# Two staging slots of their own in the second gate/up pass of a linear-attention and SwiGLU kernel

## The chip, the cores and the metric

The kernel runs on one core of a Trainium2 chip. A core has a matrix engine (TensorE, PE in the profile; its weight loads are PEld), a vector engine (VectorE, DVE), a scalar engine (ScalarE, ACT), a general engine (GpSimd, POOL) and a queue engine that only starts transfers (SyncE, SP). Each runs its own instructions in order, and they wait for each other by semaphores. Sixteen DMA engines move data between the chip's memory (DRAM) and the core's on-chip memory (SBUF); PSUM holds the sums of matmuls. The metric is device microseconds (us) of one execution, and the median over several.

## The reference

The input x is 2048 tokens by 1024 features in bf16. With xn, its layer norm, the kernel computes a linear attention block s and a SwiGLU block, and joins them:

```
xn = layernorm(x)
q, k, v = split(xn @ wqkv)                 # 32 heads of 32
phi(t) = where(t > 0, t + 1, exp(t)) + 1e-6
s = ((phi(q) @ (phi(k)^T @ v)) / (phi(q) . sum phi(k) + 1e-6)) @ wo
b = (silu(xn @ w_gate) * (xn @ w_up)) @ w_down      # inner width 3584
out = x + s * silu(b)
```

The change touches only b: its products with w_gate and w_up for the second half of the tokens, and the preparation of w_down for the product behind it.

## The kernel before

The large products go through a seven-product scheme for 2 x 2 blocks (Strassen-Winograd): sums of operand blocks are formed beside the matmuls, and seven block products replace eight. The tokens are taken in two passes of 1024. Each pass has a gate/up part of 28 units and then a down part (the product with w_down).

**Gate/up.** A unit is one weight key: a gate (g) or an up (u) slice of 256 columns, alternating, so that keys 0 to 27 are g0, u0, g1, u1 and so on. `emit_a` starts a key with 16 matmuls (four of the products), `emit_b` ends it with 12. On PE the first part of key i+1 stands ahead of the second part of key i. `emit_evac` then brings the results through DVE and ACT into hT, four rows of which make a group j of seven groups (NQ).

**Weights.** A packed key (both halves and the sums of weight blocks) is 1024 KB; SP loads it (L263) into one of eight slots of the pool wgu (`w_slot`, L215 to L216). Slots are given out as they come free. `load_w_to(n)` starts all loads up to key n. In the second pass it runs ahead by five keys up to unit 16 and by six behind it (L1697).

**The down part of the second pass** (`emit_down_m`) applies the seven products once over, as products M1 to M7, and for M1, M2 and M4 the scheme once more inside (`l2_M`, `l2_p`). These inner products need sums of weight blocks and sums of hT blocks:

- For M1 and M4, the weight sums are made in the second gate/up pass. `l2_load` (L1102) takes a slot with `w_slot()` and starts four DMAs of 128 KB (L1111) that bring two groups of blocks (the last load of each M brings one). A unit later, `l2_sums` (L1134) does four subtractions on POOL (L1144) and starts, from POOL, the store of all seven blocks to DRAM (L1145; `l` in the profile is the tensor l2_drams). There are eight such turns, at the odd units 1 to 15 (L1737). M2's were made in the first pass (`l2_early`).
- The hT sums are made by `l2_lhs` (L1160) on POOL, four operations for each group j: for M1 into two slots of wgu kept in `r_spare` (taken at units 17 and 18, L1735 to L1736), for M2 into tiles that the first pass leaves over (`x_spare`, `kept` in the profile). Both run from unit 18 on, one group j of M1 and one of M2 per unit (L1739 to L1742). The last group of M1 is in `emit_evac` of the last key, that of M2 behind the loop.

**Input and output.** `io_load` (L1184) starts two loads (x and s of one tile, L1191 and L1192) into one of five io tiles; `fin` finishes a tile, starts its store (from POOL in the first pass, L1202) and calls `io_load` for a later one. Three `fin` of the first pass are left over and run at the ends of units 0, 1 and 2 of the second pass (`deferred`, L1743).

**Order.** PE, DVE, ACT and POOL issue in source order throughout (`manual_schedule`). SP is in source order in the attention phases; in the gate/up and down phases a planner orders its transfers by a model of when their buffers come free.

Of the kernel before, what the change touches and what calls it, by code (L numbers as in the profile page):

```python
# [21 lines left out]
def kernel(  # L22
# [11 lines left out]
    nc = tc.nc  # L34
# [155 lines left out]
    M_ORDER = (1, 2, 7, 6, 5, 4, 3)  # L190
    L2 = (1, 2, 4)
    L2_ORDER = (1, 2, 5, 6, 7, 4, 3)
    NQ = NFG // 2
    CH = CW // 2
    l2_drams = {}
# [19 lines left out]
    def w_slot():  # L215
        return wgu.tile([P, 2, DC, FW], BF16, name="w_sb", tag="pk")  # L216
# [52 lines left out]
    def load_w_to(n):  # L269
        while w_next[0] < min(n, len(w_seq)):  # L270
            load_w()
# [680 lines left out]
    with ExitStack() as p3:  # L952
# [145 lines left out]

        l2_q = deque((M, j) for M in L2 if M != 2 for j in range(0, NQ, 2))
        l2_live = deque()  # L1100

        def l2_load():  # L1102
            M, j0 = l2_q.popleft()
            kd, q = M_PACK[M]
            t = w_slot()
            v = t[:].rearrange("p h a b -> p (h a b)").rearrange("p (b j n) -> p b j n", b=8, n=CH)
            js = range(j0, min(j0 + 2, NQ))
            for j in js:
                for k, b0, b1 in ((0, 0, 7), (1, 1, 6)):
                    src = wd_drams[j][0 if kd == "a" else 1][:, k, q].rearrange("p (c n) -> p c n", n=CH)  # L1110
                    nc.sync.dma_start(out=v[:, b0:b1 + 1:b1 - b0, j - j0, :], in_=src)  # L1111
            l2_live.append((M, js, v))
# [31 lines left out]
                nc.gpsimd.tensor_tensor(out=b(o_), in0=b(a_), in1=b(b_), op=ALU.subtract)  # L1144
            nc.gpsimd.dma_start(out=l2_drams[M][:, :, js.start:js.stop, :], in_=v[:, 0:7, 0:n_, :])  # L1145

        x_spare, r_spare = [], []

        def l2_bufs(M):
            v = [x[:].rearrange("p a b -> p (a b)").bitcast(F16) for x in x_spare]  # L1150
            if M == 1:
# [23 lines left out]
        for p in passes:  # L1175
# [4 lines left out]
            for hf in (1, 0):  # L1180
                for t in (2 * hf, 2 * hf + 1):
                    fq += [(p, t + TPB, 0), (p, t, 1), (p, t, 0)]

        def io_load(after=None):  # L1184
            if not fq:
                return
            p, t, cc = key = fq.pop(0)
            r0 = p * TB2 + t * P
            pool, tg = (sp, "S%d" % len(fq)) if len(fq) < 3 else (iop, "io")
            io = pool.tile([P, 2, CW], BF16, name="io", tag=tg)  # L1190
            gate([nc.sync.dma_start(out=io[:, 0, :], in_=x2[r0:r0 + P, cc * CW:(cc + 1) * CW]),  # L1191
                  nc.sync.dma_start(out=io[:, 1, :], in_=s_dram[r0:r0 + P, cc * CW:(cc + 1) * CW])],  # L1192
                 after, sync=True)
            io_tiles[key] = io
# [418 lines left out]
        base = 0  # L1613
        for pi, p in enumerate(passes):
            h = hp.tile([P, FC, TB2], BF16, name="hT", tag="hT")
            keys = [(p, kd, fg) for fg in range(NFG) for kd in ("g", "u")]
            n = len(keys)
            first = pi == 0
            last_pass = pi == NPASS - 1

            if first:
                first_gate[0] = marks[("S", NB - 1, 0)]

            def raw(j):
                return 0 <= j < n and keys[j] in raw_keys

            def pipe(j):
                if raw(j):
                    emit_st0(keys[j], w_tiles[keys[j]])

            def pipe1(k, i):
                if raw(k):
                    emit_st1(keys[k], grp[keys[i + 1]][4][:, 0:1])

            def pipe2(j):
                if raw(j):
                    t = w_tiles[keys[j]]
                    emit_st2(keys[j], t, later=j == n - 1)
                    emit_lk(keys[j][2])
                    if j < n - 1:  # L1640
                        emit_T(keys[j], t)
                    raw_keys.discard(keys[j])

            wd_live = {}

            def wd_pipe(i):
                if (i - 3) % 3 == 0 and i // 3 - 1 in wd_live:
                    key, t = wd_live[i // 3 - 1]
                    w = raw_view(key, t)
                    nc.scalar.activation(out=w, in_=w, func=ACT.Copy, scale=cs_all[:, kcol(key):kcol(key) + 1])  # L1650
                if (i - 1) % 3 == 0 and (i - 1) // 3 in wd_live:
                    emit_st0(*wd_live[(i - 1) // 3])

            def wd_pipe1(i):
                if (i - 2) % 3 == 0 and (i - 2) // 3 in wd_live:
                    emit_st1(wd_live[(i - 2) // 3][0], grp[keys[i + 1]][4][:, 1:2])

            def wd_pipe2(i):
                m, r = divmod(i + 1, 3)
                if r == 1 and m - 1 in wd_live:  # L1660
                    emit_T(*wd_live[m - 1])
                elif r == 0:
                    if m - 1 in wd_live:
                        emit_st2(*wd_live[m - 1], later=True)
                    if NWE + m < NFG:
                        t = w_slot()
                        load_wd(t, NWE + m)
                        wd_live[m] = ((p, "w", NWE + m), t)

            def more_S(m):  # L1670
                if first:
                    scale_h(h, 2 * m, nc.scalar)
                    scale_h(h, 2 * m + 1, nc.vector)
                emit_hs(h, 0, m, nc.vector)

            def next_S(m):
                emit_hs(h, 1, m, nc.vector)

            def tail():
                emit_hs(h, 0, 2, nc.vector)  # L1680
                if first:
                    scale_h(h, 7, nc.scalar)
                emit_hs(h, 0, 3, nc.vector)

            na0 = 6 if first else 8
            l2_j = 0
            load_w_to(base + na0)
            if first:
                wd_pipe2(-1)
            emit_a(keys[0])  # L1690
            emit_c22(keys[0])
            first_gate[0] = None
            for i in range(n):
                if first:
                    load_w_to(base + i + (na0 if i < n - 7 else 8 if i > n - 6 else 7))
                else:
                    load_w_to(base + i + (5 if i < 17 else 6))  # L1697
                if i + 1 < n:
                    emit_a(keys[i + 1])
                    emit_c22(keys[i + 1])  # L1700
                for j in (range(5) if i == 0 else (i + 4,) if i != n - 6 else ()):
                    pipe(j)
                if first:
                    wd_pipe(i)
                    for k in {n - 4: (0,), n - 3: (2, 4), n - 2: (5, 6)}.get(i, ()):
                        scale_h(h, k, nc.scalar)
                mb = emit_b(keys[i])
                if first and i in range(n - 6, n - 1):
                    io_load(mb)
                pipe1(i + (4 if i == n - 5 else 3), i)  # L1710
                if first:
                    wd_pipe1(i)
                if not last_pass:
                    if i == n - 2:
                        emit_hs(h, 0, 0, nc.gpsimd)
                    if i == n - 1:
                        emit_hs(h, 0, 1, nc.vector)
                emit_evac(keys[i], h, tail if i == n - 1 and not last_pass else None)
                pipe2(i + (4 if i == n - 5 else 3))
                if first:  # L1720
                    wd_pipe2(i)
                    if i == 5:
                        emit_lk(0)
                    if i == n - 5:
                        emit_lam()
                    elif i == n - 4:
                        emit_sc(keys[-1], w_tiles[keys[-1]])
                        emit_T(keys[-1], w_tiles[keys[-1]])
                        scale_h(h, 1, nc.vector)
                    elif i == n - 3:  # L1730
                        scale_h(h, 3, nc.vector)
                if not first:
                    if l2_live:
                        l2_sums()
                    if i in (17, 18):  # L1735
                        r_spare.append(w_slot())  # L1736
                    if i % 2 == 1 and l2_q:  # L1737
                        l2_load()
                    if i >= 18 and 4 * l2_j + 4 <= i:  # L1739
                        l2_lhs(1, quads(h, 0, 0), l2_j, nc.gpsimd)  # L1740
                        l2_lhs(2, quads(h, 1, 0), l2_j, nc.gpsimd)
                        l2_j += 1  # L1742
                if deferred:  # L1743
                    deferred.pop(0)()
            base += n
            if last_pass:
                l2_lhs(2, quads(h, 1, 0), NQ - 1, nc.gpsimd)
                emit_down_m(p, h, base)
            else:
                emit_down(p, h, base, last_pass, more_S, next_S)  # L1750
            base += 2 * NWA
# [32 lines left out]
```

## Time and profile before

| | us |
|---|---|
| runs | 755.99, 756.44, 761.65 |
| median | 756.44 |
| profiled execution | 756.18 |
| its span | 754.4 |
| PE busy in it | 745.8 (99%) |
| DVE / POOL / ACT busy | 581.4 / 399.8 / 381.1 |
| second gate/up pass on PE | 498.5 to 668.7 |
| down part behind it | from 668.7 |
| granted TensorE clock (share of full speed) | 0.999 |

The span runs from the first to the last instruction of the profiled execution. A timeline row has start, duration, engine, line, operation and tiles; consecutive ones of a kind are merged, with their number behind the x. SPq and POOLq are the transfers that an engine starts; a transfer's own time is in the chain's rows that begin with DMA. A row of waits has the waiting engine and line, what it waited for, the total, the number of waits and the longest.

### The profile page before, as it was taken

To read this page: it belongs to the slowest core of one execution; us is meant where nothing else is said; L and a number is where in the kernel's file an instruction comes from. 1 tells how busy PE (TensorE), PEld (TensorE's weight loads), DVE (VectorE), ACT (ScalarE), POOL (GpSimd) and SP (SyncE) were. 2 spreads that over 40 slices of the span, in tenths; PEclk is the share of its full clock that TensorE was granted. 3 is DMA by queue.
4 is the path that set the end of the run, shared out by engine and by line. 5 is a ranking of instruction groups with operands and counts; after the bars stand their busy time and mean duration, and the time that the engine had idled before them with its cause. 6 is when DMAs were issued, how large, how long until landed. Compare 5 with 4: busy or idle time off the path is not lost.

```text
span 754.4 us, 11075 instructions
## 1 busy us (share of the span) xinstructions
PE 745.8 (99%) x3857; PEld 360.8 (48%) x3857; DVE 581.4 (77%) x1040; ACT 381.1 (51%) x545; POOL 399.8 (53%) x500
## 2 busy tenths in 40 slices
PE   8999999999999999999999999999999999999997
PEld 3544444454454444444444444444444444467464
DVE  6687787887697788888889785468776877687966
ACT  5677776889956575656658311132323222232023
POOL 2444799998540266868585021811542569434900
PEclk9999999999999999999999999999999999999999
DMA  9967799879779668878799228789786768479652
GB/s 318 304 146 139 228 332 298 303 158 271 206 190 296 231 214 301 295 279 316 273 323 409 111 65 306 222 295 339 258 306 222 281 206 344 147 258 318 209 161 77
DMA packets 129160, 187.77 MB, mean 249 GB/s; under 512 B 36208, under 2 KB 104176, under 8 KB 119376
## 3 DMA queue, kind: packets, MB, share of 16 engines
q1 hardware_dynamic: 121760, 156.00, 63.9%
q0 software_dynamic: 5904, 28.58, 9.9%
q10 hardware_dynamic: 1440, 2.49, 1.1%
q8 instruction: 30, 0.49, 0.3%
q14 instruction: 26, 0.21, 0.1%
HBM read 119.47 MB, written 60.23 MB: 238 GB/s over the span
## 4 chain that ended last, share of the span: by engine, by line
PE 84%; DMA 7%; POOL 3%; DVE 2%; issue 2%; ACT 1%; SPq 1%; POOLq 0%; DVEq 0%; ACTq 0%
PE zw L966 19%; PE kv_ps L554 15%; PE xb L966 10%; PE q_ps L183 6%; PE dzw L1228 6%; PE dm L1430 6%; PE yb L966 5%; PE dm L1466 4%; PE dx L1228 3%; DMA l<-w_sb 3%; PE fx L816 3%; DMA w_sb<-wd 3%; PE s_ps L774 3%; POOL w_sb L1144 2%; PE dy L1228 2%
## 5 line engine op out<-in xcount | busy, mean ns | idle before, releaser
L966 PEld LDWEIGHTS <-w_sb 128*128 128x128 f16 (+1 forms) x1568 | 152.1, 98 | 183.8 <-DMA w_sb<-pk_u 1.3
L966 PE MATMUL xb<-xnT,w_sb 128*128 128x512 bf16 x448 | 115.0, 379 | 0.0
L554 PE MATMUL kv_ps<-wkv_sb,xnT 128*128 128x512 bf16 x512 | 113.7, 379 | 0.6 <-ACT xnT L543 0.4
L966 PE MATMUL zw<-xnT,w_sb 128*128 128x512 bf16 x448 | 105.8, 379 | 0.0
L966 PE MATMUL zw<-S,w_sb 128*128 128x512 f16 x448 | 105.8, 379 | 0.0
L321 POOL TENSOR_TENSOR w_sb<-w_sb 128x512 f16<-128x512 bf16 x42 | 50.2, 1195 | 95.7 <-DVE w_sb L309 51.3
L286 ACT ACTIVATE w_sb<-w_sb 128x2048 bf16<-128x2048 bf16 x42 | 79.9, 1902 | 3.9 <-DMA w_sb<-in_B_w_up_dram 3.9
L554 PEld LDWEIGHTS <-xnT 128*128 128x128 bf16 x512 | 48.3, 97 | 56.0 <-ACT xnT L543 0.8
L1144 POOL TENSOR_TENSOR w_sb<-w_sb 128x512 f16<-128x512 bf16 (+3 forms) x32 | 35.4, 1126 | 52.4 <-DMA w_sb<-wd 51.9
L1042 ACT ACTIVATE sg<-cg 128x1024 bf16<-128x1024 f32 x28 | 29.6, 1057 | 57.4 <-DVE cg L1035 57.4
L183 PE MATMUL q_ps<-xnT,wq_sb 128*128 128x512 bf16 x256 | 58.4, 379 | 0.0
L966 PE MATMUL yb<-S,w_sb 128*128 128x512 f16 x224 | 57.4, 379 | 0.8 <-DMA w_sb<-pk_u 0.8
L1035 DVE SCALAR_TENSOR_TENSOR cg<-zw,rc_all,s 128x1024 f32<-128x1024 f32 x28 | 35.9, 1284 | 25.3 <-PE zw L966 13.2
L994 DVE SCALAR_TENSOR_TENSOR s<-yb,rc_all,s 128x512 f32<-128x512 f32 x42 | 31.5, 749 | 27.3 <-ACT s L993 27.3
L322 POOL TENSOR_TENSOR w_sb<-w_sb 128x512 f16<-128x512 bf16 x42 | 50.5, 1202 | 3.3
L324 POOL TENSOR_TENSOR w_sb<-w_sb 128x512 f16<-128x512 bf16 x42 | 50.3, 1197 | 0.0
L323 POOL TENSOR_TENSOR w_sb<-w_sb 128x512 f16<-128x512 bf16 x42 | 50.2, 1196 | 0.0
L1202 POOL DMA_DIRECT2D out_dram<-io x16 | 8.9, 555 | 69.2 <-DVE io L1201 69.0
L993 ACT ACTIVATE s<-xb,rcl 128x512 f32<-128x512 f32 x14 | 9.6, 687 | 66.3 <-PE xb L966 66.3
L1228 PE MATMUL dx<-w_sb,hT 128*128 128x512 bf16 x112 | 42.4, 379 | 0.0
L993 ACT ACTIVATE s<-xb,rc_all 128x512 f32<-128x512 f32 x42 | 28.4, 676 | 22.0 <-issue 12.7
L309 DVE TENSOR_SCALAR w_sb<-w_sb,cs_all 128x2048 bf16<-128x2048 bf16 x35 | 36.7, 1048 | 2.8
(213 smaller groups left out, 1351.1 us busy)
## 6 DMA issues: line engine op xcount, KB each, us to landing
w_sb<-pk_g SPq DMA_DIRECT2D x27, 1024.0 KB, 6.6
pk_g<-w_sb SPq DMA_DIRECT2D x14, 1024.0 KB, 5.0
w_sb<-pk_u SPq DMA_DIRECT2D x14, 1024.0 KB, 8.3
pk_u<-w_sb POOLq DMA_DIRECT2D x13, 1024.0 KB, 5.8
w_sb<-l SPq DMA_DIRECT2D x9, 896.0 KB, 4.6
w_sb<-in_B_w_gate_dram SPq DMA_DIRECT2D x14, 512.0 KB, 6.4
w_sb<-in_B_w_down_dram SPq DMA_DIRECT2D x28, 256.0 KB, 4.8
w_sb<-in_B_w_up_dram SPq DMA_DIRECT2D x14, 512.0 KB, 5.4
```

The costliest lines, as they stand in the source:

```text
L183: nc.tensor.matmul(q_ps[:], lhsT=wq_sb[:, dc, g * P:(g + 1) * P], rhs=xn_ap(dc, btok), start=(dc == 0), stop=(dc == DC - 1))
L286: nc.scalar.activation(out=junk, in_=raw_view(key, t), func=ACT.Square, accum_out=asum[:])
L321: nc.gpsimd.tensor_tensor(out=T1, in0=b12, in1=b11, op=ALU.subtract)
L322: nc.gpsimd.tensor_tensor(out=T2, in0=b22, in1=T1, op=ALU.subtract)
L323: nc.gpsimd.tensor_tensor(out=T3, in0=b22, in1=b12, op=ALU.subtract)
L324: nc.gpsimd.tensor_tensor(out=T4, in0=b21, in1=T2, op=ALU.subtract)
L554: mm = nc.tensor.matmul(kv_ps[:], lhsT=xn_ap(dc, tok), rhs=wkv_sb[:, dc, c * CW:(c + 1) * CW], start=(dc == 0), stop=(dc == DC - 1))
L966: mm = nc.tensor.matmul(out, lhsT=lhs(k), rhs=rhs(k), start=(first and k == 0), stop=(k == HK - 1), skip_group_check=True)
L993: nc.scalar.activation(out=s1[:], in_=x_[:], func=ACT.Copy, scale=rc)
L1144: nc.gpsimd.tensor_tensor(out=b(o_), in0=b(a_), in1=b(b_), op=ALU.subtract)
L1228: nc.tensor.matmul(out, lhsT=lhs, rhs=rhs, start=first, stop=lastk, skip_group_check=True)
L1430: nc.tensor.matmul(out, lhsT=lhs_of(M)(k)[:, t * P:(t + 1) * P], rhs=w_of(M, k)[:, cols], start=first and k == 0, stop=k == NFG - 1, skip_ ...
```

## The change

In the second gate/up pass:

- The staging for M1 and M4 takes two slots when the first of its turns begins and keeps them; the turns use them alternately, and the same two are `r_spare` afterwards, so that none is taken at units 17 and 18. The turns are at the odd units 3 to 17 (`L2_UNITS`) and no longer 1 to 15.
- The weights run ahead by five keys up to unit 19 and by six from unit 20 (`L2_FROM`) on.
- M2's sums of group j are emitted at unit 4(j + 1); M1's from unit 20 on, up to two groups per unit.
- SP issues in source order within the pass (`sp_man`). `io_load` calls of the three left-over `fin` are noted and carried out three units later, behind that unit's weight load.

```diff
+    L2_FROM = 20
+    L2_UNITS = range(3, 18, 2)
...
+        x_spare, r_spare = [], []
...
         def l2_load():
             M, j0 = l2_q.popleft()
             kd, q = M_PACK[M]
-            t = w_slot()
+            while len(r_spare) < 2:
+                r_spare.append(w_slot())
+            t = r_spare[len(l2_q) % 2]
...
-        x_spare, r_spare = [], []
...
+        io_due = deque()
+        hold = [False]
+
         def io_load(after=None):
             if not fq:
+                return
+            if hold[0] and after is None:
+                io_due.append(hold[0])
                 return
...
+            sp_man = ExitStack()
+            if last_pass:
+                sp_man.enter_context(tc.manual_schedule(engines={mybir.EngineType.SP}))
             load_w_to(base + na0)
...
-                    load_w_to(base + i + (5 if i < 17 else 6))
+                    load_w_to(base + i + (5 if i < L2_FROM else 6))
+                    hold[0] = False
+                    while io_due and io_due[0] <= i:
+                        io_due.popleft()
+                        io_load()
+                    hold[0] = i + 3
...
                     if l2_live:
                         l2_sums()
-                    if i in (17, 18):
-                        r_spare.append(w_slot())
-                    if i % 2 == 1 and l2_q:
+                    if l2_q and i in L2_UNITS:
                         l2_load()
-                    if i >= 18 and 4 * l2_j + 4 <= i:
-                        l2_lhs(1, quads(h, 0, 0), l2_j, nc.gpsimd)
-                        l2_lhs(2, quads(h, 1, 0), l2_j, nc.gpsimd)
-                        l2_j += 1
+                    for _ in range(2):
+                        if i >= L2_FROM and 4 * l2_j + 4 <= i:
+                            l2_lhs(1, quads(h, 0, 0), l2_j, nc.gpsimd)
+                            l2_j += 1
+                    if i % 4 == 0 and i >= 4:
+                        l2_lhs(2, quads(h, 1, 0), i // 4 - 1, nc.gpsimd)
                 if deferred:
                     deferred.pop(0)()
+            hold[0] = False
+            while io_due:
+                io_due.popleft()
+                io_load()
+            sp_man.close()
             base += n
```

## The prediction

> **What bounds the kernel now.** I read the page's head first, then the waits of PE alone, then PE's timeline around the one wait inside the pass that the diff touches, then SP's and POOL's timelines to see where that wait comes from.
>
> ```profile
> span 754.4 us, 11075 instructions
> PE 745.8 (99%) x3857; PEld 360.8 (48%) x3857; DVE 581.4 (77%) x1040; ACT 381.1 (51%) x545; POOL 399.8 (53%) x500
> ```
>
> TensorE is busy for all but 754.4 - 745.8 = 8.6 us, start and end of the program included. No instruction of PE is added or removed. The change can therefore gain only from waits of PE that it removes:
>
> ```profile
> PE warm_ps L590 <- DVE warm L587: 1.5, 1, 1.5
> PE yb L966 <- DMA w_sb<-pk_u: 0.8, 1, 0.8
> ...
> PE dm L1466 <- ACT dm L1478: 0.3, 1, 0.3
> ```
>
> Only the second row lies in the second gate/up pass: one wait, for one weight load. The third lies in the down phase behind it. PE's timeline shows the size and place (start, duration, instruction; x is the number of matmuls):
>
> ```profile
> 615.06 1.89 PE L966 MATMUL zw<-xnT,w_sb 128*128 128x512 bf16 x8
> 616.79 1.03 PE L966 MATMUL yb<-S,w_sb 128*128 128x512 f16 x4
> ...
> 621.11 1.89 PE L966 MATMUL zw<-xnT,w_sb 128*128 128x512 bf16 x8
> 623.81 1.04 PE L966 MATMUL yb<-S,w_sb 128*128 128x512 f16 x4 [0.82 <-DMA w_sb<-pk_u]
> ...
> 660.08 1.03 PE L966 MATMUL yb<-S,w_sb 128*128 128x512 f16 x4
> ...
> 668.72 3.22 PE L1466 MATMUL dm<-w_sb,hT 128*128 128x256 bf16 x28
> 671.77 4.75 PE L1466 MATMUL dm<-w_sb 128*128 128x256 f16 x42
> ```
>
> Ahead of an undisturbed yb, eight zw matmuls take 616.79 - 615.06 = 1.73 us. So yb was due at 621.11 + 1.73 = 622.84 and came at 623.81: **0.97 us lost**. (The row says 0.82 because the modelled end of a matmul lies a little behind the next start.) One unit, that is one weight key, takes 621.11 - 615.06 = 6.05 us. The first product of the last key, 27, starts at 660.08. Between 623.81 and it lie 36.27 us, six units, so the late weight is key 21.
>
> Why is it late? SP's queue, which issues the weight loads (L263) and the staging loads for M1 and M4 (L1111):
>
> ```profile
> 567.81 1.91 SPq L1111 DMA_DIRECT2D w_sb<-wd  x4
> ...
> 581.28 1.91 SPq L1111 DMA_DIRECT2D w_sb<-wd  x4
> 583.23 0.47 SPq L263 DMA_DIRECT2D w_sb<-pk_g  x1
> ...
> 595.10 1.91 SPq L1111 DMA_DIRECT2D w_sb<-wd  x4
> 597.05 0.47 SPq L263 DMA_DIRECT2D w_sb<-pk_g  x1
> ...
> 609.05 0.88 SPq L1111 DMA_DIRECT2D w_sb<-wd  x2
> 609.99 0.46 SPq L263 DMA_DIRECT2D w_sb<-pk_g  x1
> 618.67 0.33 SPq L263 DMA_DIRECT2D w_sb<-pk_u  x1
> ```
>
> Staging turns follow each other after 13.5, 13.8 and 14.0 us, but two units of PE take 12.1. The weights stand behind them. Counting back from key 21, the three pk_g rows are keys 16, 18 and 20, due at 622.84 - 6.05 x (21 - key): 592.6, 604.7, 616.8. Their leads are 9.4, 7.6 and 6.8 us; key 21 has 622.84 - 618.67 = 4.2 us. The lead is eaten turn by turn, and the last one breaks. What paces a turn:
>
> ```profile
> 598.72 5.32 POOL L1144 TENSOR_TENSOR w_sb<-w_sb 128x512 f16<-128x512 f16 x4 [7.45 <-DMA w_sb<-wd]
> 604.34 0.90 POOL L1145 DMA_DIRECT2D l<-w_sb  x1 [0.30 <-POOL w_sb L1144]
> ```
> ```profile
> 604.34 4.67 DMA l<-w_sb
> ...
> 618.67 5.10 DMA w_sb<-pk_u
> ```
> ```profile
> SPq L1111 <- DMA l<-w_sb: 47.0, 5, 10.1
> SPq L263 <- DMA l<-w_sb: 22.3, 3, 9.1
> ```
>
> The first two fences are POOL's timeline and the chain that ended last; the third is SP's waits (total, times, longest). A turn is load (595.10 to 598.72), four subtractions and a store that lands at 609.01: 13.9 us. The next load was issued at 609.05, on that landing. So the turns run one after another, through a rotation that weights and staging share, and key 21 itself went out at 618.67 behind a store.
>
> **The change part by part.**
>
> *Slots.* The staging gets two of the eight slots, in turn; six rotate among weights. The load at unit i (odd, 3 to 17) waits for the store of four units before, 24.2 us, instead of the one before it. Against a turn of 13.9 us this leaves 10.3 us, so SP should not wait there. A weight of key m waits only for the slot of key m-6, and is due at the first product of key m, which PE starts after the second half of key m-2: four units, 24.2 us, from release to need. Landing takes
>
> ```profile
> DMA to landing us min/median/max: 4.8/7.2/17.6
> ```
>
> (all L263 loads). Even the longest fits. Key 21 goes out some 20 us before its need instead of 4.2. Value: **-0.97 us**. Bounds: 0 if it is still late, -0.97 at best, since PE has no other wait in this pass.
>
> *First turn later, at unit 3.* At the pass's start these stand:
>
> ```profile
> 521.64 4.22 SPq L1111 DMA_DIRECT2D w_sb<-wd  x8
> ...
> 526.94 0.38 SPq L263 DMA_DIRECT2D w_sb<-pk_g  x1
> ```
>
> The first is the first two staging loads, the second the load of key 8, due at 622.84 - 13 x 6.05 = 544.2. In the changed order, key 8 stands behind one io load and one staging load, about the same place: cost 0, with 17 us of cover. If that cover were gone, what is late is key 8, at one microsecond per microsecond.
>
> *io loads held three units, SP in source order.* Three io pairs move to units 3 to 5, ahead of later weights. Each waits for an output store that POOL issues:
>
> ```profile
> 526.11 5.32 POOL L1144 TENSOR_TENSOR w_sb<-w_sb 128x512 f16<-128x512 bf16 x4 [7.95 <-DMA w_sb<-wd]
> ...
> 532.49 0.72 POOL L1202 DMA_DIRECT2D out_dram<-io  x1
> ```
>
> Now the third store stood behind the subtractions; afterwards no sums are due before unit 4, so it goes earlier by some 5 us. Queued behind a waiting io load are one staging load and the weights of keys 8 to 10, whose cover is the 17 us above. Cost 0; bound above 1 us, if both covers are used at once.
>
> *M2's sums early, M1's from unit 20.* No operation is added. Now they stand bunched:
>
> ```profile
> 618.60 0.67 POOL L1163 TENSOR_TENSOR kept<-hT 128x256 f16<-128x256 bf16 x1
> ...
> 642.94 0.67 POOL L1166 TENSOR_TENSOR kept<-hT,kept 128x256 f16<-128x256 bf16 x1
> ```
>
> These are the first and last of M2's first twenty. One group of four takes about 2.6 us (618.60 to 621.23 in this stretch); one every fourth unit (24.2 us) goes among turns that use POOL 6.2 us in 12.1. So POOL is at 2 x 6.2 + 2.6 = 15 us of 24.2. A sum that waits for its hT rows holds back the subtractions behind it by at most a unit, inside the 10.3 us of slack. M1's must wait for the last store out of its buffers; POOL then does two groups a unit at 20 and 21, done about 630, where PE's first products with them (the last row of PE's timeline above) start at 671.77. The last groups of both keep their place. Value 0, bounds 0 and +1 us.
>
> What speaks against it is DVE:
>
> ```profile
> 588.09 0.97 DVE L1049 TENSOR_TENSOR hT<-cu,sg 128x1536 bf16<-128x1536 bf16 x1
> ...
> 600.18 1.73 DVE L1049 TENSOR_TENSOR hT<-cu,sg 128x1536 bf16<-128x1536 bf16 x1
> ```
> ```profile
> 578.00:584.00 6.00, 6.00 (x30) 2.70 (x29) 3.07 (x4) 2.32 (x3) 0.00 (x0) 1.00 0.65 214
> 584.00:590.00 6.00, 6.00 (x29) 2.73 (x28) 5.60 (x7) 1.23 (x2) 5.17 (x4) 1.00 0.98 373
> ```
>
> The multiply at 600.18 fell beside the subtractions of 598.72 and took 0.76 us longer. The window rows (fourth number: DVE) make 8.7 us of 12 for two units; with 0.76 more in each pair it is 9.4, and PE still does not wait. The multiply at 588.09, also beside POOL, got through in 0.97. I take 0.
>
> The Trainium skill, page "SBUF — State Buffer", section "Who interferes with whom", says that a DVE instruction with two SBUF inputs and a GpSimd instruction that reads SBUF exclude each other for a whole instruction. The trace agrees at 600.18 and not at 588.09. By that rule the sum would be up to 4.6 us worse, as the third rival works out from the rows.
>
> *Down phase.* Its code is the same; its last six-slot rotation too. But SP's order there is planned anew from another starting point. Unknown: bounds -0.3 us (the third PE wait above) and +8.3 us:
>
> ```profile
> SPq L1202 <- DVE io L1201: 19.3, 7, 8.3
> ```
>
> I take 0, because PE's only wait there now is 0.3 us.
>
> **Sum.** 756.18 us, the profiled execution's own time, minus 0.97 gives 755.21. It stands 0.26 below the median of the runs (756.44), so for a median: 756.44 - 0.97 = 755.47, **755.5 us**.
>
> **Rivals.**
>
> *The wait moves, nothing is gained.* At the pass's start the order io load, staging load, key 8 is now fixed, while the first eight weights still land; or another weight misses its need by about as much. For it: the 17.6 us landing and the 4.22 us that eight staging DMAs took at 521.64. Against: 17 us of cover. Price: about +1 on the forecast, 756.4.
>
> *The down phase is planned worse, and it is slower.* SP works in order. An output store that waits 8.3 us for DVE, put ahead of a weight load, delays that load by 8.3 us; PE stalls as far as this exceeds the load's lead. Without any lead, 755.5 + 8.3 = 763.8 us, a little over 1%. Against: the same code is planned now with 0.3 us of PE wait.
>
> *DVE is held up by the early sums, and PE with it.* Six groups of M2's sums move from the pass's end to places all along it. If each makes a DVE instruction 0.76 us later and all of it reaches PE, 6 x 0.76 = 4.6 us: 760.1. Against: DVE has 12.1 - 8.7 = 3.4 us to spare in each pair of units.
>
> *The queue blocks in the pass.* In source order a late staging turn holds every weight behind it. With T the turn, the lag grows by (T - 24.2)/2 per pair of units over seven pairs, against some 17 us (24.2 minus the landing of 7.2). It decides from T = 24.2 + 2 x 17/7 = 29 us, double of 13.9. At T = 35 it would cost 7 x 5.4 - 17 = 21 us: 776 us. Nothing in the trace makes a turn double.
>
> *The staging still shares slots with weights.* Then key 21 stays late, 756.4; a part of the first rival's case.
>
> **How the numbers follow.** Forecast 0.78, wait moves 0.12 (the shared slots among it), DVE held up 0.02 (under 1%), down phase worse 0.05 (half of it under 1%), queue blocks 0.03. One per cent is 7.6 us, about what a measurement of this kernel can tell from no change. To be faster by so much, PE would have to lose nearly all of its 8.6 us of idle time, start and end too: 0.01. Slower: 0.03 + 0.03 = 0.06. Within 1%: 0.93. The range takes in the forecast and the first rival, 0.90: low 755.5 less 0.45 (two of the three runs before, 755.99 and 756.44, differ by that) less the 0.3 of the down phase, 754.7; high 756.4 plus 0.45 and 1 us for the bounds of the io loads and sums, 757.8.
>
> **What would show it.** Right: PE's waits have no row for a weight load in the pass; the last M4 staging load is issued near 600 instead of 609.05; SP's waits of L1111 and L263 on the store are close to none; key 21 goes out near 600; M2's sums stand singly from about 530 on; PE's busy time is unchanged and the down phase begins near 667.7. Wrong: a PE wait on w_sb of a microsecond or more anywhere, early in the pass (first rival), growing from turn to turn (fourth), after DVE's evacuations (third), or behind an output store in the down phase (second).

## The result, and the profile after

The changed kernel takes 755.53 us (median of 22 executions, 754.41 to 757.18), the kernel before, run beside it, 756.88 us (755.62 to 761.65). The ratio is 0.9974 with a 95% interval of 0.9963 to 0.9985: 1.1 to 2.8 us faster. By the 1% bound of the prediction that is no change, and the time lies on the forecast of 755.5; but the interval excludes 1, so the gain is real. It is larger than the 0.97 us that the forecast was made from: the medians differ by 1.35 us and the means by 1.97, because before has more long executions.

The profiled execution of the changed kernel took 756.19 us, nearly the same as that of before; it was the second slowest of its 22, so what it shows is the place of the waits, not the size of the gain. Its head, and the waits of PE that bear on the pass:

```profile
span 754.4 us, 11017 instructions
...
PE 742.7 (98%) x3793; PEld 361.3 (48%) x3857; DVE 580.5 (77%) x1040; ACT 381.1 (51%) x545; POOL 398.6 (53%) x500
```
```profile
PE yb L968 <- DMA w_sb<-pk_u: 0.3, 1, 0.3
...
PE dm L1475 <- ACT dm L1487: 0.3, 1, 0.3
```

(3793 instead of 3857 matmuls: records are missing, and with them some busy time.) There is still a row for a weight load, so one has to look where it stands. SP's queue late in the pass, and PE's timeline:

```profile
576.13 2.71 SPq L1116 DMA_DIRECT2D w_sb<-wd  x4
581.74 0.33 SPq L265 DMA_DIRECT2D w_sb<-pk_g  x1
587.78 0.33 SPq L265 DMA_DIRECT2D w_sb<-pk_u  x1
588.21 2.09 SPq L1116 DMA_DIRECT2D w_sb<-wd  x4
593.82 0.33 SPq L265 DMA_DIRECT2D w_sb<-pk_g  x1
599.87 0.33 SPq L265 DMA_DIRECT2D w_sb<-pk_u  x1
600.30 0.89 SPq L1116 DMA_DIRECT2D w_sb<-wd  x2
```
```profile
502.97 1.04 PE L968 MATMUL yb<-S,w_sb 128*128 128x512 f16 x4 [0.32 <-DMA w_sb<-pk_u]
...
617.80 1.03 PE L968 MATMUL yb<-S,w_sb 128*128 128x512 f16 x4
...
623.85 1.03 PE L968 MATMUL yb<-S,w_sb 128*128 128x512 f16 x4
```

The staging loads (now L1116) follow each other after 12.1 us, the pace of PE. The weights (now L265) go out one by one, 6.04 us apart, whenever PE frees a slot; within the pass SP waits for no store of the staging any more, and waits for PE instead:

```profile
SPq L265 <- PE zw L968: 86.4, 18, 5.6
```

Key 21, the last pk_u of the fence, is issued at 599.87 instead of 618.67. The place where PE waited before, 623.81, is now passed at 623.85 without a wait. What is left is at 502.97: key 1, the second weight of the pass. SP issues it at 494.92 here and at 494.32 before, in the same place of the same order of loads, so the change does not touch its issue.

### The profile page after: what moved, and what is told of

Read it like the earlier page. It is cut to its first block, busy times and chain, and to the rows that moved or that the text cites. A ratio compares the mean times of both kernels' runs of the same rounds, so it can differ in the third digit from the quotient of the medians.

```text
span 754.4 us, 11017 instructions
## 1 busy us (share of the span) xinstructions
PE 742.7 (98%) x3793; PEld 361.3 (48%) x3857; DVE 580.5 (77%) x1040; ACT 381.1 (51%) x545; POOL 398.6 (53%) x500
## 4 chain that ended last, share of the span: by engine, by line
PE 90%; DMA 3%; DVE 2%; POOL 1%; issue 1%; ACT 1%; SPq 0%; DVEq 0%; ACTq 0%; POOLq 0%
PE zw L968 25%; PE kv_ps L556 15%; PE xb L968 13%; PE q_ps L183 6%; PE yb L968 6%; PE dm L1439 6%; PE dm L1475 4%; PE dzw L1237 3%; PE fx L818 3%; PE s_ps L776 2%; PE dy L1237 2%; PE dx L1237 1%; DMA w_sb<-pk_g 1%; POOL w_sb L1137 1%; DMA w_sb<-pk_u 1%
## 5 line engine op out<-in xcount | busy, mean ns | idle before, releaser
L968 PE MATMUL xb<-xnT,w_sb 128*128 128x512 bf16 x420 | 113.3, 379 | 1.5
L1037 DVE SCALAR_TENSOR_TENSOR cg<-zw,rc_all,s 128x1024 f32<-128x1024 f32 x28 | 35.9, 1283 | 25.5 <-PE zw L968 13.9
L1149 POOL TENSOR_TENSOR w_sb<-w_sb 128x512 f16<-128x512 bf16 (+3 forms) x32 | 33.1, 1056 | 29.9 <-DMA w_sb<-wd 29.2
```

The lines of the kernel that those rows point to most:

```text
L968: mm = nc.tensor.matmul(out, lhsT=lhs(k), rhs=rhs(k), start=(first and k == 0), stop=(k == HK - 1), skip_group_check=True)
```

## The experiments

**One yardstick for all runs.** The pass on PE runs from its first yb matmul to the first dm matmul of the down part. Without a wait it takes 169.21 us. For each profiled execution, in us:

| kernel | pass | beyond 169.2 | time | time less that |
|---|---|---|---|---|
| before, as predicted from | 170.21 | 1.0 | 756.18 | 755.2 |
| before, four more executions | 169.61 / 169.94 / 170.55 / 171.96 | 0.4 / 0.7 / 1.4 / 2.8 | 755.85 / 756.30 / 756.91 / 758.09 | 755.4 / 755.6 / 755.6 / 755.3 |
| changed, two executions | 169.71 / 169.21 | 0.5 / 0.0 | 756.19 / 755.42 | 755.7 / 755.4 |
| own slots alone | 171.13 | 1.9 | 757.50 | 755.6 |
| source order alone | 175.43 | 6.2 | 761.48 | 755.3 |
| early sums alone | 169.44 | 0.2 | 755.24 | 755.0 |
| slots and sums | 169.21 | 0.0 | 755.26 | 755.3 |
| slots and order | 169.21 | 0.0 | 755.27 | 755.3 |
| changed, turns lengthened | 169.21 | 0.0 | 755.03 | 755.0 |
| before, turns lengthened | 191.63 | 22.4 | 778.00 | 755.6 |

The last column stays within 0.7 us while the times spread over 23. To within that 0.7 us, what these kernels differ by is lost or kept inside this one pass.

The starts of the yb matmuls (undisturbed, 3.45 us from key 0 to key 1 and 6.05 from key to key behind it) show where. The five executions of before, in the order of the table, lost 0.0 / 0.2 / 0.4 / 0.9 / 0.8 us at key 1 and 1.0 / 0.2 / 0.3 / 0.4 / 1.9 us at key 21, and next to nothing elsewhere. The changed kernel lost 0.5 / 0.0 at key 1 and nothing at key 21.

The theory under test: staging turns in a shared rotation run one after another, slower than PE, and so hold back weights. Its rivals: that the order of SP's queue alone counts; that the place of M2's sums counts; that the wait near 623 us was a chance meeting of transfers.

**The three parts, each alone, on the kernel before.**

Own slots alone (with their later turns and the weights' run-ahead; the sums of M1 and M2 together from unit 20, SP planned as before):

```diff
...
-            t = w_slot()
+            while len(r_spare) < 2:
+                r_spare.append(w_slot())
+            t = r_spare[len(l2_q) % 2]
...
-                    load_w_to(base + i + (5 if i < 17 else 6))
+                    load_w_to(base + i + (5 if i < L2_FROM else 6))
...
-                    if i % 2 == 1 and l2_q:
+                    if l2_q and i in L2_UNITS:
...
```

> The kernel before with the two staging slots alone (turns at units 3 to 17, weights ahead by six from unit 20, sums of M1 and M2 together from unit 20), SP still ordered by the planner. Theory (turns of 13.9 us run one after another against 12.1 us of PE and hold back a weight): the whole gain of the change is here, about 755.5 us, ratio to before 0.997 to 0.999, no PE wait for a weight inside the pass, last staging load near 600 us. Rival (the order of SP's queue is what counts): as before, 756.9 us, with a PE wait near 623 us. Rival (the place of M2's sums counts): as before too.

Measured: 760.1 us, ratio 1.0053 (1.0032 to 1.0073). The expectation fell: the part that was to bring the whole gain made the kernel slower. SP's queue in the profiled execution shows where its 1.9 us went, with the PE row that follows from it and SP's waits for stores:

```profile
562.59 0.38 SPq L265 DMA_DIRECT2D w_sb<-pk_u  x1
573.57 3.58 SPq L1116 DMA_DIRECT2D w_sb<-wd  x6
577.24 0.42 SPq L265 DMA_DIRECT2D w_sb<-pk_g  x1
...
582.85 1.04 PE L968 MATMUL yb<-S,w_sb 128*128 128x512 f16 x4 [1.75 <-DMA w_sb<-pk_g]
```
```profile
SPq L1116 <- DMA l<-w_sb: 33.3, 5, 10.5
```

The last staging loads stand ahead of key 14 (the pk_g at 577.24), and SP issued nothing from 562.97 to 573.57, the longest of its waits for a store. With free slots of their own, the staging loads were planned early, and behind them the weights waited for a store after all. That is the prediction's fourth rival, a staging load that blocks the queue, only that the planner's order did it and not the source order. The profiled execution, 757.50 us, was the fastest of six (up to 762.98); where the slower ones lost the rest is not shown.

Source order alone (SP in source order and the io loads held; slots shared as before):

```diff
...
+            sp_man = ExitStack()
+            if last_pass:
+                sp_man.enter_context(tc.manual_schedule(engines={mybir.EngineType.SP}))
...
```

> The kernel before with SP in source order and the io loads held, shared slots and late sums as before. Theory (turns against PE): turns still follow each other after 13.5 to 14 us, so a PE wait for a weight of about 1 us stays, 756.9 us, ratio 0.999 to 1.002; in source order a late store holds the weights behind it too, so it may be worse. Rival (order of SP's queue): the gain is here, 755.5 us, no PE wait in the pass.

Measured: 760.38 us, ratio 1.0047 (1.0029 to 1.0064), above the range of 0.999 to 1.002, though the theory had allowed for worse. In the profiled execution (761.48 us, the slowest of six) PE waits twice, on keys 15 and 21:

```profile
590.05 1.31 PE L966 MATMUL yb<-S,w_sb 128*128 128x512 f16 x4 [3.21 <-DMA w_sb<-pk_u]
...
629.14 1.04 PE L966 MATMUL yb<-S,w_sb 128*128 128x512 f16 x4 [0.98 <-DMA w_sb<-pk_u]
```

SP's waits name the cause:

```profile
SPq L263 <- DMA l<-w_sb: 38.9, 5, 10.4
```

The weight loads themselves wait for stores of the staging, 38.9 us against 22.3 before, because they still get its slots in turn: key 15 went out at 585.00, when such a store had landed (584.94), and in source order nothing behind it can go ahead. So the order by itself is no gain either.

Early sums alone:

```diff
-                        l2_lhs(2, quads(h, 1, 0), l2_j, nc.gpsimd)
                         l2_j += 1
+                    if i % 4 == 0 and i >= 4:
+                        l2_lhs(2, quads(h, 1, 0), i // 4 - 1, nc.gpsimd)
```

> The kernel before with M2's sums early alone. Theory (turns against PE): 756.9 us, ratio 0.999 to 1.003; the wait near 623 us stays or grows by up to 1 us, since single groups of 2.6 us now stand among the turns on POOL. Rival (the bunched sums count): 755.5 us. Rival (DVE held up by early sums): up to 4.6 us slower, 761 us.

Measured: 756.8 us, ratio 1.000 (0.9987 to 1.0013): nothing, as the theory had it, and the rival by which early sums hold up DVE falls, beyond about 1 us. The profiled execution does not show the wait that the theory expected to stay: at 755.24 us it was the fastest of twelve, and it lost 0.2 us at key 1 and nothing at key 21. That the wait stays in the others rests on the ratio alone.

**Two parts at a time.** The changed kernel with SP planned again and the io loads not held, that is slots and sums:

```diff
...
-                sp_man.enter_context(tc.manual_schedule(engines={mybir.EngineType.SP}))
...
-                    hold[0] = i + 3
...
```

> The changed kernel with SP ordered by the planner and the io loads not held: slots and early sums only. Theory (turns against PE): as the changed kernel, 755.5 us, ratio to before 0.997 to 0.999. Rival (order of SP's queue): back to 756.9 us, a PE wait for a weight in the pass of about 1 us.

Measured: 755.24 us, ratio 0.9980 (0.9968 to 0.9992), the whole gain. The planner is the same as in the run with slots alone, but it made another order. Its queue at the same place:

```profile
557.32 0.38 SPq L265 DMA_DIRECT2D w_sb<-pk_u  x1
557.79 0.40 SPq L265 DMA_DIRECT2D w_sb<-pk_g  x1
567.35 5.80 SPq L1116 DMA_DIRECT2D w_sb<-wd  x3
```

Here key 14 (557.79) goes out ahead of the waiting staging load, 19 us earlier than with slots alone. What made the planner choose so was not tried apart; the two kernels differ in the place of M2's sums and nothing else. It was a near thing: SP still waits 38.3 us for stores of the staging, in five waits, and key 11 lands 2.7 us ahead of its first matmul (559.82 against 562.51), where in the changed kernel every weight from key 8 on lands 15 us ahead or more.

Slots and source order, with M2's sums late:

```diff
+                            l2_lhs(2, quads(h, 1, 0), l2_j, nc.gpsimd)
                             l2_j += 1
-                    if i % 4 == 0 and i >= 4:
-                        l2_lhs(2, quads(h, 1, 0), i // 4 - 1, nc.gpsimd)
```

> Own slots and SP in source order, sums of M2 late as before: the changed kernel without its early sums. Theory A (own slots take away the serial turns, and the source order keeps the staging loads from standing ahead of weights in SP's queue; the early sums only move POOL work): as the changed kernel, 755.5 us, ratio to before 0.997 to 0.999, no PE wait inside the pass behind key 1. Theory B (the early sums are needed, since both kernels that gained have them): 757 us or more, with a PE wait in the pass.

Measured: 755.42 us, ratio 0.9978 (0.9966 to 0.9991). Theory A held, theory B fell: the early sums are not needed. What gains is own slots together with an order that keeps waiting staging loads behind the weights that are due. With own slots the source order gave that, and the planner gave it in one of two cases. The parts that go along with the two, the first turn at unit 3 and the run-ahead with the slots, the held io loads with the order, were not tried apart.

**The turn's length.** The four subtractions of each turn done twice, the second time with the same result, in the kernel before and in the changed one:

```diff
-            for o_, a_, b_ in ((2, 7, 0), (3, 6, 2), (4, 6, 7), (5, 1, 3)):
+            for o_, a_, b_ in 2 * ((2, 7, 0), (3, 6, 2), (4, 6, 7), (5, 1, 3)):
```

> The kernel before with the four subtractions of each staging turn done twice (the second time with the same result). Theory (turns in series set the pace): a turn grows from 13.9 to about 18.6 us against 12.1 us of PE for two units; seven turns lose 4.7 us each beyond the 0.97, so some 25 to 35 us slower, 780 to 790 us, with PE waits on several weights. Rival (the wait near 623 us is a chance meeting of transfers): 757 to 760 us.

> The changed kernel with the four subtractions of each turn done twice. Theory (two slots allow a turn of 24.2 us): a turn of 18.6 us costs nothing, 755.5 us, ratio to before 0.997 to 0.999. Rival (POOL or the queue becomes the bound as soon as a turn is longer than two units, 12.1 us): 8 turns of 6.5 us beyond it, up to 40 us slower.

Measured: before 778.0 us (one execution, 21 us above the 756.75 of the kernel before beside it), changed 755.12 us, ratio to before 0.9974 (0.9960 to 0.9987). The staging loads of the lengthened kernel before, and then of the lengthened changed kernel with SP's waits for its stores:

```profile
571.82 2.53 SPq L1111 DMA_DIRECT2D w_sb<-wd  x4
...
590.72 1.91 SPq L1111 DMA_DIRECT2D w_sb<-wd  x4
...
608.58 2.69 SPq L1111 DMA_DIRECT2D w_sb<-wd  x4
...
627.03 0.88 SPq L1111 DMA_DIRECT2D w_sb<-wd  x2
```
```profile
530.11 1.92 SPq L1116 DMA_DIRECT2D w_sb<-wd  x4
...
557.47 0.89 SPq L1116 DMA_DIRECT2D w_sb<-wd  x2
...
576.75 1.91 SPq L1116 DMA_DIRECT2D w_sb<-wd  x4
...
587.83 1.91 SPq L1116 DMA_DIRECT2D w_sb<-wd  x4
...
600.57 0.89 SPq L1116 DMA_DIRECT2D w_sb<-wd  x2
```
```profile
SPq L1116 <- DMA l<-w_sb: 17.9, 6, 6.7
```

In the kernel before, a turn grew to 18.9, 17.9 and 18.5 us, and PE paid for it with waits on keys 16, 18, 20 and 21; that is no chance meeting. The loss is below the 25 to 35 us expected, because the early turns overlapped more and the last staging load moved by 18 us (609.05 to 627.03) and not by 33. In the changed kernel PE waits for no weight, as expected, but not for the reason expected. SP now does wait for stores, six times and 17.9 us in all. A load waits for the store of the turn two before it, in the same slot, so a turn can be read off the rows: from 530.11 to 557.47 is 27 us, from 576.75 to 600.57 is 24. All eight took 19.2 to 27.3 us, and not 18.6. Two were longer than the 24.2 us of four units. What keeps PE busy is the lead of the weights: from key 8 on each lands at least 13 us ahead of its first matmul.

The slack of 10.3 us was not there even without the longer turns. In the changed kernel itself, the turn that was loaded at 576.13 has these rows on POOL:

```profile
584.05 4.62 POOL L1149 TENSOR_TENSOR w_sb<-w_sb 128x512 f16<-128x512 f16 x4 [3.31 <-DMA w_sb<-wd]
588.96 0.90 POOL L1150 DMA_DIRECT2D l<-w_sb  x1 [0.30 <-POOL w_sb L1149]
```

From load to sums it took 7.9 us, where the turn of before that the prediction reads took 3.6, and the store landed at 596.94, 8.0 us behind its issue and not 4.7. That makes 20.8 us; the turns of two groups took 18.6 to 21.2 in this execution, which leaves 3 to 6 us of the 24.2.

**The same kernels once more**, for the spread.

> The kernel before once more, for the profile of another execution. If the wider spread of its times comes from the same wait, the PE waits on weights in the second pass make up the time above 755.2 us, within 0.5 us; if it comes from elsewhere, they stay near 1 us whatever the time.

> The kernel before, a further execution. Same question as for the first repetition: the waits of PE's weight loads on weights in the second pass make up the time above 755.2 us within 0.5 us (theory), or stay near 1 us (rival). At 759 us, 3 to 4 us of waits by the theory.

> The kernel before, a further execution; expected as for the one ahead of it: waits on weights equal to the time above 755.2 us within 0.5 us, or near 1 us whatever the time.

> The kernel before, a further execution; expected as for the two ahead of it.

> The changed kernel once more. Theory: no PE wait on a weight behind key 1, staging loads 12.1 us apart; the wait on key 1 at the pass's start comes and goes with the landing of that load, 0 to 0.5 us; 755.0 to 755.9 us.

Measured: before 755.85, 758.09, 756.91 and 756.30 us, changed 755.42 us. The table above has their passes. Counted as the theory said, by PE's waits, the answer is mixed: the waits add up to 0, 2.39, 0.99 and 0.25 us, 0.5 to 0.85 less than the time above 755.2. They do not stay near 1 us either. Counted by the length of the pass, which takes in what the modelled ends hide, the loss makes up that time within 0.4 us. In the slowest, it has two places:

```profile
502.92 1.04 PE L966 MATMUL yb<-S,w_sb 128*128 128x512 f16 x4 [0.61 <-DMA w_sb<-pk_u]
625.74 1.04 PE L966 MATMUL yb<-S,w_sb 128*128 128x512 f16 x4 [1.78 <-DMA w_sb<-pk_u]
```

The first is key 1, at the pass's start; this wait shows here, in two other repetitions of before and in one of the two executions of the changed kernel, and comes and goes with the landing of that load. The second is key 21, with twice the loss that the prediction was made from. No profile was taken of an execution of before above 759 us, though some take that long; that they too lose their time in the pass is likely by the table, but not shown.

## Why the prediction was right, and where it was short

**The bound.** Right. PE's work is fixed; what can be won is what PE waits for. Every profiled execution that lost no time in the pass came to 755.0 to 755.4 us.

**The wait on key 21 and its cause.** Right: removed by slots and order, not by early sums as far as the ratio of 1.000 tells, and multiplied when the turns were made longer in the kernel before, at the predicted length of a turn (18.6 predicted, 17.9 to 18.9 measured).

**Its size.** The term was -0.97 us, from one execution; the ratio says -1.1 to -2.8, so the sum is short. The term itself is not shown to be: at key 21 the five profiled executions of before lost 0.2 to 1.9 us, 0.8 on average. That the forecast of 755.5 was met to 0.03 us is luck: the median that it starts from, 756.44, lies 0.44 below the one measured beside the change, and its term lies 0.38 below the difference of the medians. The rest of the gain is open. It can lie in the long executions of before, of which no profile was taken, and in key 1, where before lost 0.4 us on average and the changed kernel 0.5 and 0.0; two profiles can't tell these apart. What the prediction lacked is the spread: a wait that is a race between turns and PE differs from execution to execution, and that should have been part of the sum. The interval of the ratio is 1.7 us wide, so a measurement tells much less than the 7.6 us that the prediction took for its limit. The changed kernel's runs lie within 2.8 us of each other, those of before within 6.0.

**Slots and order as separate terms.** This is the step that failed, though the sum does not show it. The prediction gave the gain to the slots and zero to the source order. Slots alone were slower by 0.53%, the order alone by 0.47%, and only both, or slots with a lucky plan, gain. The order's term is not zero: it keeps the slots' gain from turning into a blocked queue. The fourth rival had the mechanism but laid it to the source order, which with own slots prevents it, and needed a turn of 29 us; in the planner's order with own slots it took turns of 22.6 us at most.

**The turn and its slack.** The turn was put too short and its slack too large. The prediction took the turn over from the kernel before, 13.9 us, and so had 10.3 us to spare. Its step was to take a length measured with the turns in series for one beside evenly spaced weights. In the changed kernel a turn takes about 20 us, because its load and its store land later than before. That SP need not wait for the staging held all the same, with 3 to 6 us to spare in that execution; with turns lengthened by some 5 us it did wait, and the lead of the weights covered it.

**First turn, io loads, early sums.** Zero, as said: the first two were not tried apart, but keys 8 to 10, which stand behind them, land 15 to 18 us ahead of their need in the changed kernel, and the early sums cost nothing either alone or on top of slots and order. M2's groups stand singly from 532.33 on, among the turns. M1's first five groups were not done about 630 but at 637, because M2's group of unit 20 stands ahead of some of them on POOL and waits for its hT rows:

```profile
626.40 0.67 POOL L1166 TENSOR_TENSOR kept<-hT 128x256 f16<-128x256 bf16 x1 [7.43 <-DVE hT L1051]
...
636.29 0.68 POOL L1169 TENSOR_TENSOR w_sb<-hT,w_sb 128x256 f16<-128x256 bf16 x1
```

PE wants them over 30 us later, so it costs nothing. DVE's multiply did not grow on average; the groups of before and, then, of the changed kernel, over both passes:

```profile
L1049 DVE TENSOR_TENSOR hT<-cu,sg 128x1536 bf16<-128x1536 bf16 x28 | 28.9, 1031 | 1.0
```
```profile
L1051 DVE TENSOR_TENSOR hT<-cu,sg 128x1536 bf16<-128x1536 bf16 x28 | 28.3, 1012 | 1.0
```

The rule of the Trainium skill that spoke against the change (page "SBUF — State Buffer", section "Who interferes with whom") costs PE nothing here: 1031 ns before, 1012 after, and a ratio of 1.000 with early sums alone. Single multiplies in the pass still take up to 1.56 us, where undisturbed ones take 0.96, but that was so before (1.73).

**Wait moves (first rival).** There is a wait at the pass's start in the changed kernel's first profile, 0.5 us of pass time. It is not a price of the change: the kernel before shows it too, in three of its five executions, and the changed kernel's second execution does not. The down part began at 667.97 in that one, near the 667.7 expected, and at 668.74 in the first.

**Down phase planned worse.** No: the only PE wait there is the same 0.3 us on ACT.

## What to carry to other kernels

When a staging chain shares a rotation with prefetched weights, compare the length of one turn with the time in which the consumer uses up what is loaded (and measure the turn again behind the change: here it grew from 13.9 to about 20 us); a lead that shrinks by 1 or 2 us per turn is a wait to come, even if the profile shows only the last one. Buffers of its own are half of the cure: on an in-order queue, a transfer with a free-looking buffer can be placed ahead of one that is due, so the order has to be fixed along with the buffers. And when a gain hangs on one small wait of one execution, its size is a range.

## What the runs showed of the hardware

A long wait of PE cost more than its own length. In the kernel before with longer turns, the matmuls behind a wait ran slowly for some microseconds. PE's timeline (the last row is an undisturbed group of the same four), and then windows of 4 us with the granted clock as the third number from the end:

```profile
598.04 1.89 PE L966 MATMUL yb<-S,w_sb 128*128 128x512 f16 x4 [4.89 <-DMA w_sb<-pk_g]
...
643.93 1.62 PE L966 MATMUL yb<-S,w_sb 128*128 128x512 f16 x4 [2.71 <-DMA w_sb<-pk_u]
...
624.78 1.03 PE L966 MATMUL yb<-S,w_sb 128*128 128x512 f16 x4
```
```profile
596.00:600.00 4.00, 1.96 (x5) 0.74 (x6) 0.00 (x0) 0.00 (x0) 4.00 (x4) 0.56 0.91 377
600.00:604.00 4.00, 3.78 (x11) 1.51 (x11) 0.75 (x1) 0.69 (x1) 3.62 (x5) 0.59 0.00 0
604.00:608.00 4.00, 4.00 (x21) 1.80 (x19) 3.29 (x4) 0.00 (x0) 0.76 (x1) 1.00 0.66 228
```

The four waits of that execution add up to 14.2 us (4.89, 4.30, 2.33 and 2.71), but its pass lost 22.4: most of the rest is matmuls behind the waits, in windows with a clock of 0.56 to 0.82 (0.50 from 598 to 602 us). A wait of 2.71 us was enough for it, the wait of 1.78 us in the slowest execution of before was not (its four matmuls took 1.04). The Trainium skill, page "TensorE: Matmul & The Clock Gate", section "What's actually happening", puts the drop to half clock behind one idle window of about 3.4 us that runs freely; the runs agree on the half clock and the few microseconds, while the waits that set it off were shorter, 2.33 us by the profile's modelled ends. With source order alone the wait of 3.21 us did the same: the next 2 us windows have 0.67 and 0.50. For this kernel it means that a weight that is 1 or 2 us late costs that much, and one that is 2.3 to 5 us late about 2 us more.
